# First channel product of six chunks by Strassen's algorithm, and reciprocals through rings, in an attention and mixer kernel

## The chip, the core and the metric

The kernel runs on one core of one Trainium2 chip. Its engines work side by side, each on its own list of instructions in order: PE (TensorE) multiplies matrices into the banks of PSUM, DVE (VectorE), ACT (ScalarE) and POOL (GpSimd) work on tiles, and SP issues transfers, as ACT and POOL do too. The time is device microseconds (us) of one execution; the number compared is the median of several.

## The reference

Eight batches of 576 positions by 8 heads of 64 go through an attention whose kernel is a random feature map, and then through a mixer over tokens and over channels.

```python
def phi(x):
    h = np.einsum('bhsd,md->bhsm', x, omega) - np.sum(x * x, axis=-1, keepdims=True) / 2.0
    return np.exp(h - np.max(h, axis=-1, keepdims=True)) / np.sqrt(m)
kv  = np.einsum('bhsm,bhsd->bhmd', phi(k_s), v)
z   = np.sum(phi(k_s), axis=2)
x   = einsum(phi(q_s), kv) / (einsum(phi(q_s), z) + 1e-06)      # attention, 8 x 576 x 512

u   = x + (np.maximum(xT @ w_tok1, 0.0) @ w_tok2)T              # tokens: 576 -> 256 -> 576
out = u + np.maximum(u @ w_ch1, 0.0) @ w_ch2                    # channels: 512 -> 1536 -> 512
```

## The kernel before

**Tiling.** Of a batch's 576 positions 512 are its main part; the 64 that are left of each of the eight batches make up a ninth chunk of 512, the tail. The channel part runs over nine chunks c: the batches 0 to 7 and the tail (c = B). Everything on PE is fp16 and is summed in fp32 in eight banks of 128 x 512.

**Order.** No scheduler decides at run time. The code adds jobs (an engine, a function, the jobs it waits for, the ring places it takes and gives back) to a `Planner`, and `ORDER`, a list of job numbers written out in the file, says in which order they are issued. `SLOT` gives the ring place (a bank, a buffer) for each job that takes one, `MOVED` the jobs that run on another engine than the usual one, and negative numbers in `ORDER` are matmuls on zeros at the start. So each engine's list, and what a ring place waits for, is fixed.

**Stages of a batch.** `load_transposed` casts q and k on POOL's queue into scratch memory and brings them back transposed on SP's queue into a place of the rings qT and kT (three each). `attention` projects k and q on PE (L656, L668), takes the exponential on ACT (L514), the maximum over features and its reciprocal on DVE (L680, L682), multiplies v by it on POOL (L295, `vs`), and forms the product of k's features and v (L701 to L710) and from it, for each head, numerator and denominator (L734, L736). One job (`num_out`) then takes the reciprocal of the denominator and scales the head into x (L743, L744); for two heads of batch 0 the scaling is on ACT instead (L756). `token_mix` makes two products with a relu between them (L777, L790) and adds x (L793); u is transposed by a transfer on SP's queue into uT (`ut_dma`, L798). The tail's rows are added for pairs of batches in `token_tail` (L850) and transposed into uTt.

**Channel part.** `channel_mix` makes the first product directly: for each of 12 blocks of 128 of the 1536 channels, 4 matmuls of 512 columns into one bank (L966), and a relu of that bank to fp16 (L290 on ACT, L292 on DVE). The second product is direct for batch 0 (L1000). For the other chunks `channel_out_fast` makes it by Strassen's algorithm in Winograd's form: four sums of quarters of the relu's output on DVE (L295, tiles S and r), four differences of quarters of the weights made once (T1 to T4), seven products of 24 matmuls of 256 columns (L916), and adds that read the banks into the output tile (L905), which a store then sends out (L945, L952).

Helpers that the profile names by their own lines: `copy` (L286), `relu_to` (L290, L292), `tt` (L295).

Of the kernel before, what the change touches and what calls it, by code (L numbers as in the profile page):

```python
# [9 lines left out]
FP32 = mybir.dt.float32  # L10
# [158 lines left out]
def kernel(  # L169
# [12 lines left out]
    nc = tc.nc  # L182
# [888 lines left out]
```

## Time and profile before

| | |
|---|---|
| Time, median of 3 | 276.59 us (276.38, 276.59, 277.32) |
| Span of the profiled execution, first to last instruction | 275.9 us |
| Instructions | 6228 |
| First product of the tail and most batches (L966), one matmul as the profile models its end | 379 ns |
| Bytes moved by transfers | 39.66 MB |

Only the span of the profiled execution is known, not its time as it is measured from outside; the difference to the median is 0.7 us. The profile gives the busy time of each engine, the same in stretches of time, groups of equal instructions (a line of the kernel, an engine, tiles without their numbers, shapes, a count, busy time and mean duration of one, and the idle time before them with what ended it), and the chain that ended last: from the last instruction back, at each step, to what released it. Matmuls are pipelined, so the duration of one is longer than the distance from one to the next.

### The profile page before, as it was taken

Reading aid. Unit: us, or ns where it says so; the run is one execution under the profiler, and the core shown is the slowest. Engines: PE = TensorE matmul, PEld = TensorE weight load, DVE = VectorE, ACT = ScalarE, POOL = GpSimd, SP = SyncE. Lnnn points to the kernel's source line nnn. Section 1 sums busy time; section 2 is a strip of 40 time slices with the busy share of each in tenths; the row PEclk is TensorE's granted clock in tenths of the full one; section 3 lists DMA queues with packets and bytes.
Section 4 is the critical chain, followed back from the end, with each engine's and each line's share of the span. In section 5 each row is a group of like instructions: output and inputs, shape, how many; then the busy total and the mean of one; then the engine's idle time right before and its main releaser. Section 6 shows DMA issues by size and latency. Waiting matters only on the chain.

```text
span 275.9 us, 6228 instructions
## 1 busy us (share of the span) xinstructions
PE 266.6 (97%) x2503; PEld 165.5 (60%) x2503; DVE 222.9 (81%) x462; ACT 138.1 (50%) x289; POOL 91.2 (33%) x115
## 2 busy tenths in 40 slices
PE   8789999999999999999999999999999999999993
PEld 3367455444567655755676656755676477446782
DVE  3897889876998799987999899978985992675992
ACT  3999941188685338734756456636654500040200
POOL 8994492063703490075019510600043000000001
PEclk9999999999999999999999999999999999999998
DMA  7999999999998999979989994840252304021125
GB/s 195 192 209 212 190 212 177 202 193 146 203 191 133 229 176 186 151 148 171 198 184 183 232 125 123 191 90 2 97 79 77 96 0 95 2 99 53 78 83 146
DMA packets 81292, 39.66 MB, mean 144 GB/s; under 512 B 63984, under 2 KB 77040, under 8 KB 81072
## 3 DMA queue, kind: packets, MB, share of 16 engines
q0 software_dynamic: 31744, 17.74, 44.2%
q1 hardware_dynamic: 47072, 15.50, 28.7%
q10 hardware_dynamic: 2448, 6.03, 5.6%
q8 instruction: 19, 0.31, 0.5%
q14 instruction: 9, 0.07, 0.1%
HBM read 35.95 MB, written 16.52 MB: 190 GB/s over the span
## 4 chain that ended last, share of the span: by engine, by line
PE 89%; DMA 6%; POOL 3%; DVE 0%; issue 0%; POOLq 0%
PE bank L966 33%; PE bank L916 25%; PE bank L777 5%; PE bank L790 5%; DMA w1m<-in_moe_w_tok_dram 4%; PE bank L1000 4%; PE bank L734 3%; PE bank L656 3%; PE bank L668 2%; PE bank L701 2%; DMA uT<-u 2%; POOL r L319 1%; PE bank L844 1%; PE bank L816 1%; PE bank L828 1%; PE bank L736 1%
## 5 line engine op out<-in xcount | busy, mean ns | idle before, releaser
L966 PE MATMUL bank<-uT,wc 128*128 128x512 f16 x376 | 90.4, 379 | 0.3 <-DMA uT<-u 0.3
L290 ACT ACTIVATE r<-bank 128x512 f16<-128x512 f32 (+1 forms) x84 | 46.9, 597 | 77.1 <-PE bank L966 62.0
L295 POOL TENSOR_TENSOR vs<-v,vs 128x512 f16<-128x512 f16 x31 | 33.2, 1074 | 91.2 <-DVE vs L682 60.5
L966 PEld LDWEIGHTS <-wc 128*128 128x128 f16 x424 | 38.3, 98 | 37.9 <-issue 1.1
L916 PEld LDWEIGHTS <-r 128*128 128x128 f16 x384 | 36.9, 98 | 8.1 <-issue 1.2
L514 ACT ACTIVATE kp<-bank 128x512 f16<-128x512 f32 x64 | 35.6, 622 | 10.4 <-PE bank L656 10.4
L514 ACT ACTIVATE qp<-bank 128x512 f16<-128x512 f32 x64 | 36.3, 616 | 8.9 <-PE bank L668 6.0
L680 DVE TENSOR_REDUCE km<-kp 128x8 f16<-128x1024 f16 x32 | 38.6, 1206 | 2.5 <-ACT kp L514 2.4
L292 DVE TENSOR_SCALAR r<-bank 128x512 f16<-128x512 f32 (+1 forms) x42 | 27.7, 672 | 12.0 <-PE bank L966 11.2
L744 DVE TENSOR_TENSOR x<-bank,rc 128x320 f16<-128x320 f32 x62 | 30.5, 492 | 2.1
L916 PEld LDWEIGHTS <-S 128*128 128x128 f16 x288 | 27.9, 98 | 5.4 <-issue 0.3
L905 DVE TENSOR_TENSOR o<-u,bank 128x512 f32<-128x512 f16 x28 | 19.0, 679 | 6.9 <-PE bank L916 6.8
L916 PE MATMUL bank<-T,r 128*128 128x256 f16 x192 | 23.8, 273 | 0.0
L916 PE MATMUL bank<-T,S 128*128 128x256 f16 x192 | 23.6, 273 | 0.0
L916 PE MATMUL bank<-wc,r 128*128 128x256 f16 x192 | 23.6, 273 | 0.0
L945 POOL DMA_DIRECT2D out_dram<-o x2 | 1.3, 648 | 60.9 <-issue 60.9
L793 DVE TENSOR_TENSOR u<-x,bank 128x512 f16<-128x512 f16 x28 | 17.8, 681 | 1.1 <-PE bank L790 1.0
L905 DVE TENSOR_TENSOR o<-o,bank 128x512 f32<-128x512 f32 (+1 forms) x27 | 16.6, 618 | 2.2 <-PE bank L916 1.6
L734 PEld LDWEIGHTS <-qp 128*128 128x128 f16 x256 | 13.8, 98 | 7.0 <-DVE kvsb L286 0.2
L734 PE MATMUL bank<-kvsb,qp 128*128 128x65 f16 x256 | 15.6, 193 | 0.0
L743 DVE RECIPROCAL rc<-bank 128x5 f32<-128x5 f32 x62 | 11.5, 186 | 4.1 <-PE bank L736 2.7
L701 PEld LDWEIGHTS <-kp 128*128 128x128 f16 x256 | 11.5, 98 | 5.1
(120 smaller groups left out, 376.3 us busy)
## 6 DMA issues: line engine op xcount, KB each, us to landing
out_dram<-o ACTq DMA_DIRECT2D x9, 512.0 KB, 2.6
q<-in_q_dram POOLq DMA_DIRECT2D x6, 576.0 KB, 7.2
wc<-in_moe_w_ch_dram POOLq DMA_DIRECT2D x4, 768.0 KB, 10.6
k<-in_k_dram POOLq DMA_DIRECT2D x6, 512.0 KB, 6.9
v<-in_v_dram POOLq DMA_DIRECT2D x6, 512.0 KB, 8.9
out_dram<-o SPq DMA_DIRECT2D x5, 512.0 KB, 3.9
r<-in_q_dram POOLq DMA_DIRECT2D x4, 288.0 KB, 7.3
v<-in_v_dram POOLq DMA_DIRECT2D x4, 256.0 KB, 8.7
```

Source lines behind the costliest of these rows:

```text
L290: nc.scalar.activation(out=out, in_=in_, func=AF.Relu)
L292: nc.vector.tensor_relu(out=out, in_=in_)
L295: (nc.gpsimd if eng == "POOL" else nc.vector).tensor_tensor(**kw)
L514: nc.scalar.activation(out=out, in_=in_, func=AF.Exp, bias=0.0, scale=1.0)
L680: nc.vector.reduce_max(out=mx, in_=kpv, axis=AX.X)
L701: nc.tensor.matmul(ps[:, i, :], kpv[:, 2 * i + j // 2, j % 2, :], vs[:, i * NJ + j, 0 : D + 1], start=(i == 0 and j == 0), stop=False, ski ...
L734: nc.tensor.matmul(ps[:, k, j * 65 : (j + 1) * 65], st, s[:, i, 0 : D + 1], start=True, stop=True)
L744: nc.vector.tensor_tensor(out=t_x[place("x", b)][:, :, (2 * hp + hs[0]) * D : (2 * hp + hs[0] + n) * D].rearrange("p j (i d) -> p i j d", ...
L793: nc.vector.tensor_tensor(out=t_u[place("u", b)][:, j, :], in0=t_x[place("x", b)][:, j, :], in1=bank(n), op=ALU.add)
L905: nc.vector.tensor_tensor(out=o, in0=a, in1=ps, op=ALU.add)
L916: nc.tensor.matmul(ps[:, j * DH : (j + 1) * DH], a[:, cb, j * P : (j + 1) * P], w[:, cb, :], start=(bank_of(b, j0) not in held and j == j0 ...
L966: nc.tensor.matmul(ps, wc1[:, db, cb * P : (cb + 1) * P], moving(db), start=(db == 0), stop=(db == ND - 1))
```

## The change

**First product.** From batch 3 on (`FAST_IN = 3`), and for the tail, the first channel product is made by Strassen's algorithm too. The two operands are split in quarters: channels in halves of 768, the 512 inputs in halves of 256 (k), the 512 positions in halves of 256 (j). `weight_sums` makes four sums of quarters of wc1 once, before batch 3's channel part; six of their eight halves lie in one place of the qT ring and one of the kT ring, which they hold to the end, two in a new tile. For each chunk four differences of quarters of uT are made into another place of uT's ring. For each of three groups of two blocks, seven products of four matmuls of 256 columns go into three banks X, Y and Z. A product that others go on adding to is first kept: ACT copies the bank in fp32 to a free buffer (r3, qp or kp), and DVE joins the kept sum with another bank (L1101 of the changed kernel). The relu of three quarters is then made in place in SBUF, that of the fourth from the bank.

```diff
+    FAST_IN = 3
...
+    def weight_sums(key):
+        def quad(i, k, a):
+            return wc1[:, 2 * k + a, i * (DC // 2) : (i + 1) * (DC // 2)]
+        steps = (((1, 0), (1, 1), ALU.add), (0, (0, 0), ALU.subtract), ((0, 0), (1, 0), ALU.subtract), ((0, 1), 1, ALU.subtract))
+        for a in range(2):
+            done = []
+            for i, (x, y, op) in enumerate(steps):
+                e_sum = engine("DVE")
...
+    def channel_in_fast(c, key, jt):
...
+        steps = ((lambda: block(0, 1), lambda: block(0, 0)), (lambda: block(1, 1), lambda: sums()[:, 0]), (lambda: block(1, 1), lambda: block(0, 1)),
+                 (lambda: block(1, 0), lambda: sums()[:, 1]))
...
+        ops = {
+            "P1": ("X", weights(0, 0), lambda: block(0, 0), []),
+            "P2": ("Y", weights(0, 1), lambda: block(1, 0), []),
+            "P5": ("Z", sum_weights(0), lambda: sums()[:, 0], [j_sums[0][0], j_sums[1][0], j_s[0]]),
+            "P6": ("X", sum_weights(1), lambda: sums()[:, 1], [j_sums[0][1], j_sums[1][1], j_s[1]]),
+            "P7": ("X", sum_weights(2), lambda: sums()[:, 2], [j_sums[0][2], j_sums[1][2], j_s[2]]),
+            "P4": ("X", weights(1, 1), lambda: sums()[:, 3], [j_s[3]]),
+            "P3": ("Z", sum_weights(3), lambda: block(1, 1), [j_sums[0][3], j_sums[1][3]]),
+        }
...
+                    for n in range(2):
+                        for a in range(2):
+                            nc.tensor.matmul(ps[:, n, :], w(a)[:, (2 * m + n) * P : (2 * m + n + 1) * P], x_[:, a],
+                                             start=(what in ("P1", "P2", "P5") and n == 0 and a == 0), stop=False, skip_group_check=True)
...
+            p1 = product("P1", [])
+            p2 = product("P2", [])
+            p5 = product("P5", [])
+            k1 = keep("P1", "X", p1)
+            c11 = join("P1", "Y", 0, 0, [k1, p2], True)
+            p6 = product("P6", [k1])
+            k2 = keep("U2", "X", p6)
+            p7 = product("P7", [k2])
+            k3 = keep("U3", "X", p7)
+            c22 = join("U3", "Z", 1, 1, [k3, p5, c11], False)
+            p3 = product("P3", [c22])
+            c12 = join("U2", "Z", 0, 1, [k2, p3], True)
+            p4 = product("P4", [k3])
...
     def channel_mix(c, key, jt):
         def moving(db):
             return (t_uT[place("uT", c)] if c < B else uTt)[:, :, db, :]
+        if c >= FAST_IN:
+            channel_out_fast(c, key, channel_in_fast(c, key, jt))
+            return
```

**Reciprocals.** What was one job is split: the maximum and its reciprocal, the reciprocal of the denominator and the scaling are jobs of their own, and their small results take places of rings (km 4, rc 8, kmt 2) instead of two fixed ones that alternate. The scaling can run on ACT for any head.

```diff
-    t_km = ring(2, [P, 8], FP16, "km")
-    t_kmt = ring(2, [P, 4], FP16, "kmt")
+    t_sum = sb([P, 2, DC // 2], FP16, "sum")
+    t_km = ring(COUNT["km"], [P, 8], FP16, "km")
+    t_kmt = ring(COUNT["kmt"], [P, 2, 4], FP16, "kmt")
-    t_rct = ring(2, [P, 4], FP16, "rct")
-    t_rc = ring(4, [P, 2, NJ + 1], FP32, "rc")
+    t_rc = ring(COUNT["rc"], [P, NJ + 1], FP32, "rc")
...
+                def rec(hp=hp, i=hs[0], where=where):
+                    nc.vector.reciprocal(out=t_rc[place("rc", (b, hp, i))], in_=where()[:, 0, 0 : 5 * 65].rearrange("p (j d) -> p j d", d=65)[:, :, D])
+                j_r = add("DVE", 0.1, kno, rec, deps=[j_n], take=[("rc", (b, hp, hs[0]))])
+                e_num = engine("DVE")
...
+                    if e_num == "ACT":
                         for j in range(NJ + 1):
+                            nc.scalar.activation(out=to[:, j], in_=ps[:, j], func=AF.Copy, scale=rc[:, j : j + 1])
+                    else:
+                        nc.vector.tensor_tensor(out=to, in0=ps, in1=rc.unsqueeze(2).broadcast_to((P, NJ + 1, D)), op=ALU.mult)
```

**Places and order.** The r1 ring has two places, not three. The tail's output is formed in places of the x ring instead of the output ring. Two more options (`SPLIT`, `HALVES`) are in the code and are empty. `ORDER`, `SLOT` and `MOVED` are new throughout; with them some sums of the second product, most sums of u and five weight sums run on POOL, eleven more heads are scaled on ACT, and the transposes of batches 5 to 7 stand at other places of SP's list.

```diff
-             "kvsb": 3, "ktt": 2, "x": 3, "r1": 3, "u": 3, "uT": 3, "r3": 2, "S": 1, "o": 2, "bank": 8}
+             "kvsb": 3, "ktt": 2, "x": 3, "r1": 2, "u": 3, "uT": 3, "r3": 2, "S": 1, "o": 2, "km": 4, "rc": 8, "kmt": 2, "bank": 8}
...
+        def o_tag(i):
+            return ("x", ("o", i)) if tail else ("o", (c, i))
```

More of the change, by code (lines that the diff above doesn't have):

```diff
@@ L104 @@
+    1318: "POOL", 1319: "POOL", 1320: "POOL", 1334: "DVE", 1351: "ACT", 1352: "ACT", 1391: "ACT", 1392: "ACT",
+    1397: "POOL", 1398: "POOL", 1430: "DVE", 1431: "ACT", 1447: "ACT",
 }
@@ L598, in kt_max @@
                 )
-            j_ktm = add("DVE", 1.2, kkt + 0.01, kt_max, deps=[*j_kte, j_msk], take=[("vbd", b)] if dma_in else [])
+            j_ktm = add("DVE", 0.15, kkt + 0.01, kt_mask, deps=[j_ktm, j_msk], take=take_vbd, give=[("kmt", b)])
             def vbd():
@@ L762, in attention @@
+                last_x.append(add(e_num, 0.45, kno, scale, deps=[j_r], take=[("x", b)], give=[at, ("rc", (b, hp, hs[0]))]))
         return last_x
@@ L865, in channel_out_fast @@
             part = slice(g * NH // 2, (g + 1) * NH // 2)
-            need = [jr[cb + NH * e] for cb in range(part.start, part.stop) for e in range(2)]
+            need = [x for cb in range(part.start, part.stop) for e in range(2) for x in jr[cb + NH * e]]
             steps = (
@@ L897, in bank_of, with o_of, go @@
             return (b, c, j0) if tail else (b, c)
+        def o_tag(i):
+            return ("x", ("o", i)) if tail else ("o", (c, i))
+        def o_of(i):
+            if tail:
+                return t_x[place(*o_tag(i))].rearrange("p j d -> p (j d)")[:, 0 : 4 * DM].bitcast(FP32).rearrange("p (j d) -> p j d", j=2)
+            return t_o[place(*o_tag(i))]
         def read(k, b, i, e, base, deps, free, j0=0, j1=2):
-            def go(c=c):
-                o = t_o[place("o", (c, i))][:, j0:j1, DH * e : DH * e + DH]
+            e_read = engine("DVE")
+            def go(c=c, e_read=e_read):
+                o = o_of(i)[:, j0:j1, DH * e : DH * e + DH]
                 ps = bank(bank_of(b, j0)).rearrange("p (j d) -> p j d", j=2)[:, j0:j1]
+                if e_read == "ACT":
+                    nc.scalar.copy(out=o, in_=ps)
+                    return
                 u = t_u[place("u", c)] if c < B else t_ut
@@ L944, in store @@
                         to = out[4 * i : 4 * i + 4, SM:S, cols].rearrange("(j h) t d -> h t j d", h=2)[h]
-                        (nc.scalar if eng == "ACT" else nc.sync if eng == "SP" else nc.gpsimd).dma_start(out=to[:, js], in_=t_o[place("o", (c, i))][half[h], js, cols])
-                    dma(eng, key + 0.9, 0.3, store, deps=[outs[need, j] for j in range(*js)], give=[("o", (c, i))],
+                        (nc.scalar if eng == "ACT" else nc.sync if eng == "SP" else nc.gpsimd).dma_start(out=to[:, js], in_=o_of(i)[half[h], js, cols])
+                    dma(eng, key + 0.9, 0.3, store, deps=[outs[need, j] for j in range(*js)], give=[o_tag(i)],
                         cost=0.412 if js[1] - js[0] == 1 else 0.414)
@@ L951, in store @@
             def store(i=i, eng=eng):
-                (nc.scalar if eng == "ACT" else nc.sync).dma_start(out=out[c, 0:SM, :].rearrange("(p j) d -> p j d", j=NJ)[:, 2 * i : 2 * i + 2, :], in_=t_o[place("o", (c, i))])
-            dma(eng, key + 0.9 + 0.1 * i, 1.3, store, deps=[outs[x, 0] for x in need], give=[("o", (c, i))], cost=0.4)
+                (nc.scalar if eng == "ACT" else nc.sync).dma_start(out=out[c, 0:SM, :].rearrange("(p j) d -> p j d", j=NJ)[:, 2 * i : 2 * i + 2, :], in_=o_of(i))
@@ new lines, in channel_out_fast, with sum_of, go @@
+            dma(eng, key + 0.9 + 0.1 * i, 1.3, store, deps=[outs[x, 0] for x in need], give=[o_tag(i)], cost=0.4)
+    j_sums = []
+    def sum_of(i, k):
+        n = 2 * i + k
+        if n < 6:
+            tag = "qT" if n < 3 else "kT"
+            return (t_qT if n < 3 else t_kT)[place(tag, "sums")][:, n % 3 * (DC // 2) : n % 3 * (DC // 2) + DC // 2]
+        return t_sum[:, n - 6]
+    def weight_sums(key):
[3 more added lines that the diff above has]
+        for a in range(2):
+            done = []
+            for i, (x, y, op) in enumerate(steps):
+                e_sum = engine("DVE")
+                def go(i=i, a=a, x=x, y=y, op=op, e_sum=e_sum):
+                    x, y = [sum_of(z, a) if isinstance(z, int) else quad(*z, a) for z in (x, y)]
+                    tt(e_sum, out=sum_of(i, a), in0=x, in1=y, op=op)
+                need = [done[z] for z in (x, y) if isinstance(z, int)]
+                n = 2 * i + a
+                done.append(add(e_sum, 0.46, key, go, deps=[*need, *j_wc1], take=[("qT" if n < 3 else "kT", "sums")] if n < 6 else []))
+            j_sums.append(done)
@@ L984, in relu @@
                 relu_to(e_relu, t_r3[place("r3", c)][:, cb, :], bank(n))
[L985 removed]
+            jr[cb] = [add(e_relu, 0.5, key + 0.5 * pos / NCB, relu, deps=[j1], take=[("r3", c)], give=[("bank", n)])]
         if fast:
```

201 lines of the change are left out of this document (144 added, 57 removed), and 132 rows, old and new, of the table ORDER.

## The prediction

> **What bounds the kernel now.** I read the page's head first, then the stretches of time, then the chain that ended last, and only then the groups.
>
> ```profile
> span 275.9 us, 6228 instructions
> ...
> PE 266.6 (97%) x2503; PEld 165.5 (60%) x2503; DVE 222.9 (81%) x462; ACT 138.1 (50%) x289; POOL 91.2 (33%) x115
> ...
> PEclk9999999999999999999999999999999999999998
> ...
> PE 89%; DMA 6%; POOL 3%; DVE 0%; issue 0%; POOLq 0%
> ```
>
> The page's head shows one engine at 97% and a chain that runs 89% over it. Whether those 97% are real work is told by the stretches (columns: PE, PEld, DVE, ACT, POOL busy us, granted clock, DMA share, GB/s).
>
> ```profile
> 0.00:10.00 10.00, 7.51 (x82) 4.08 (x82) 4.82 (x18) 5.27 (x10) 8.55 (x19) 1.00 0.91 189
> 10.00:20.00 10.00, 8.39 (x150) 4.75 (x151) 9.12 (x20) 9.67 (x28) 9.50 (x12) 1.00 1.20 207
> 20.00:30.00 10.00, 9.54 (x162) 7.06 (x155) 7.70 (x18) 9.34 (x23) 4.00 (x6) 1.00 1.22 205
> 30.00:50.00 20.00, 20.00 (x167) 10.28 (x165) 18.25 (x37) 9.61 (x21) 11.73 (x13) 1.00 1.28 192
> 50.00:70.00 20.00, 20.00 (x174) 9.93 (x172) 14.37 (x26) 13.41 (x28) 7.06 (x9) 1.00 1.09 178
> ...
> 130.00:150.00 20.00, 20.00 (x206) 13.97 (x205) 18.86 (x38) 12.13 (x26) 5.82 (x7) 1.00 1.05 186
> ...
> 270.00:276.00 6.00, 1.44 (x14) 1.05 (x11) 1.27 (x3) 0.00 (x0) 1.15 (x2) 0.82 0.51 135
> ```
>
> From 30 us on PE has no idle time until 271.4, at full granted clock; what it lacks is lost in the first 30 us and in the last 4.5, where only stores are left. A busy PE need not be an efficient one, so I took two long unbroken pieces of the chain of waits (start, us, what):
>
> ```profile
> 234.09 13.81 PE bank L966 x64
> ...
> 260.94 10.51 PE bank L916 x96
> ```
>
> 64 matmuls of 512 columns in 13.81 us are 0.2158 us each; 96 of 256 columns in 10.51 are 0.1095. Half the columns take half the time although each has its own weight load, so a matmul costs its columns and nothing else, and time can only be saved by fewer columns on PE.
>
> **The change on PE.** The direct first product (L966) is 48 matmuls of 512 columns a chunk: 48 x 0.2158 = 10.36 us. By Strassen a chunk takes 3 groups x 7 products x 4 matmuls = 84 of 256 columns: 84 x 0.1095 = 9.20. That is 1.16 us less, and for six chunks (batches 3 to 7 and the tail) 7.0 us less. PE gets nothing else new. Bounds: the moving operand is now strided over two blocks, but L966's was strided too, so I keep the row's price; if each of the 504 cost 5 ns more, 2.5 us would go.
>
> **The other engines.** The rows that price what is added and removed:
>
> ```profile
> L290 ACT ACTIVATE r<-bank 128x512 f16<-128x512 f32 x82 | 46.1, 602 | 76.6 <-PE bank L966 62.0 <-PE bank L777 8.9 <-DVE o L905 5.4
> ...
> L295 POOL TENSOR_TENSOR vs<-v,vs 128x512 f16<-128x512 f16 x31 | 33.2, 1074 | 91.2 <-DVE vs L682 60.5 <-PE bank L668 22.3 <-PE bank L966 4.5
> ...
> L744 DVE TENSOR_TENSOR x<-bank,rc 128x320 f16<-128x320 f32 x62 | 30.5, 492 | 2.1
> ...
> L292 DVE TENSOR_SCALAR r<-bank 128x512 f16<-128x512 f32 x40 | 26.9, 684 | 11.7 <-PE bank L966 11.2
> ...
> L905 DVE TENSOR_TENSOR o<-o,bank 128x512 f32<-128x512 f32 x21 | 14.1, 674 | 1.6 <-PE bank L916 1.1 <-issue 0.2
> ...
> L295 DVE TENSOR_TENSOR S<-r,S 128x768 f16<-128x768 f16 x16 | 8.5, 553 | 0.2
> ...
> L286 DVE CAST kvsb<-bank 128x130 f16<-128x130 f32 x12 | 3.4, 287 | 5.1 <-PE bank L708 5.1
> ...
> L756 ACT ACTIVATE x<-bank,rc 128x64 f16<-128x64 f32 x10 | 2.3, 340 | 0.0
> ...
> L295 POOL TENSOR_TENSOR T<-vt,T 128x1024 f16<-128x1024 f16 x1 | 1.9, 1941 | 0.0
> ...
> L286 ACT COPY o<-bank 128x512 f32<-128x512 f32 x2 | 1.3, 638 | 4.8 <-PE bank L1000 4.8
> ...
> L290 ACT ACTIVATE r<-bank 128x256 f16<-128x256 f32 x2 | 0.8, 384 | 0.4 <-PE bank L817 0.4
> ...
> L545 DVE COPY ktt<-kT 128x256 f16<-128x256 f16 x1 | 0.2, 227 | 0.0
> ```
>
> Counts come from the two instruction lists.
>
> DVE gains 54 joins of a kept product with a bank, priced as L905's add: 54 x 0.674 = 36.4; 3 relus from a bank at 0.684, 2.1; 3 weight sums at 0.553, 1.7; 6 sums of u of 512 elements, between the copy's 0.227 and 0.553, taken as 0.42 = 2.5; 10 relus in place of 512 elements and 8 of 1024, never seen: below by 0.227 each, above by 0.684 per 512 (17.8 in all); nearest are the fp16 rows, so 0.30 and 0.45 = 6.6. It loses 24 relus (16.4), 17 sums for the second product, given to POOL (9.4), 11 scalings of heads, given to ACT (5.4), and 2 casts (0.6). Net 49.3 - 31.8 = +17.5, so 240.4.
>
> ACT gains 54 keeps x 0.638 = 34.5; 15 relus at 0.602 = 9.0; 55 scalings (11 heads of 5) x 0.340 = 18.7; 8 relus in place at 0.602 and 10 of twice that size at 1.04 (0.602 plus twice the 0.218 between 256 and 512) = 15.2; 2 casts, taken at 0.287; it loses 48 relus, 28.9. Net +49, so 187.
>
> POOL gains 18 sums of u at 1.074 and 22 of 768 elements, between 1.074 and 1.941, taken half-way at 1.5: 19.3 + 33 = 52, so 143.5.
>
> Against a span near 269 these are 89, 70 and 53%. No engine overtakes PE, but DVE has much less air. How much less is a question of how the count of durations relates to time on a full engine (timeline of DVE and ACT: start, us, what):
>
> ```profile
> 106.99 0.56 DVE L295 TENSOR_TENSOR S<-r,S 128x768 f16<-128x768 f16 x1
> 107.47 0.55 DVE L295 TENSOR_TENSOR S<-S,r 128x768 f16<-128x768 f16 x1
> ...
> 108.53 0.68 DVE L793 TENSOR_TENSOR u<-x,bank 128x512 f16<-128x512 f16 x1
> 109.13 0.55 DVE L295 TENSOR_TENSOR S<-r,S 128x768 f16<-128x768 f16 x1
> ```
>
> ```profile
> 202.38 0.59 ACT L514 ACTIVATE kp<-bank 128x512 f16<-128x512 f32 x1
> 202.85 0.60 ACT L514 ACTIVATE qp<-bank 128x512 f16<-128x512 f32 x1
> ```
>
> Back to back, DVE starts the next instruction 0.08 us before the last one is through (0.48 after a 0.56, 0.60 after a 0.68), ACT 0.12 before. So durations overstate the load: the 480 or so DVE instructions need about 38 us less than their sum.
>
> **Waits that the change adds.** Four products of a group share bank X (P1, P6, P7, P4) and two bank Z: before the next one adds to a bank, ACT must have kept, or DVE joined, the last sum. In PE's new order I added up the matmuls that stand between each product and the next on its bank: at the least 0.87 us of other PE work, four places under 1.1, half of them over 2.8. A keep takes 0.638. So nearly all handoffs are covered; if the cover were gone each would cost about 0.64, and behind a waiting product stands everything in PE's queue. I count 0.3 for the thin ones.
>
> The transposes by DMA have less lead. Priced by the trace's landing times (queue, count, median us from issue to landing):
>
> ```profile
> uT<-u SPq DMA_TRANSPOSE x7, 5.4
> kT<-k SPq DMA_TRANSPOSE x6, 5.6
> qT<-q SPq DMA_TRANSPOSE x6, 6.1
> ```
>
> Six of the eight weight sums now hold one of three places of qT and of kT from before batch 5's load on, so batches 5 to 7 load later. PE work between issue and first use, counted the same way, is 5.5 us for batch 7's qT against 6.1 to land: 0.6 late. For u it was 6.0 to 8.0 and becomes 5.0 to 5.7 from batch 4 on, against 5.4: I take 0.4 in all, 0 to 2 as bounds. The first sums of u come behind that, but P1 and P2 need none.
>
> At the end, from the last transpose of u to the last matmul, PE has 43.9 us (43.3 before), DVE 79 instructions of 44.4 us (55 of 31.7 before). Less 79 x 0.08 it is 38.1, 87% of PE's. Before, DVE there waited for PE; now the last relus, sums and reads come in a close chain, with only batch 7's last 12 matmuls (1.3 us) as cover between the tail chunk's two products. I take 0.7, with 0 and 3 as bounds.
>
> **Edits at nothing.** The reciprocals and scalings are split into jobs of their own and go through rings of 4 and 8 places: the same 64 and 32 instructions, on an engine that is not on the path. The tail's output now lies in x's places: same adds, same stores. The first 70 us of PE, SP and POOL are the same but for bank numbers and a few swaps, so the head keeps its 4.6 us of idle time. r1 has two places in the room of three; in the new order each pair's tail product, which frees them, still stands ahead of the next token product, so nothing waits. What hides the split is the air of DVE above; without it the instructions would still be the same ones, and only their order on a full DVE would count (the first rival).
>
> **The sum.** 275.9 - 7.0 + 0.3 + 0.6 + 0.4 + 0.7 = 270.9 of span. The median shown is 276.59, 0.7 over this execution's span, and I keep that difference: **271.6 us**.
>
> **A rule that speaks against it.** POOL's sums and DVE's run side by side now (timelines of DVE and of POOL):
>
> ```profile
> 14.52 1.02 DVE L295 TENSOR_TENSOR vs<-v,vs 128x512 f16<-128x512 f16 x1
> ```
>
> ```profile
> 13.39 1.05 POOL L295 TENSOR_TENSOR vs<-v,vs 128x512 f16<-128x512 f16 x1 [0.47 <-DVE vs L682]
> ...
> 14.96 1.50 POOL L295 TENSOR_TENSOR vs<-v,vs 128x512 f16<-128x512 f16 x1
> ```
>
> The one POOL multiply that ran into a DVE one with both inputs in SBUF took 1.50 instead of 1.05. The Trainium skill, "GPSIMD Engine Reference", section "Key points", says that POOL shares its SBUF interfaces with VectorE and is held up by DVE instructions with two SBUF inputs; the trace agrees, 0.45 us for 0.58 of overlap. In the sum: 77 adds on POOL, 0.45 each at worst, are 35 us on an engine with 125 to spare; it moves no term, only the lateness of sums, which is the third rival.
>
> **Rivals.**
> - **DVE becomes the bound.** Busy DVE time is 54.3 up to 70 us and 168.6 after; with 17.5 more it is 186.1 for the 199 us left, 93.5%. The densest row above, 130 to 150, reached 94.3%. If dependences hold it to 92%, the rest takes 202.3: 70 + 202.3 + 0.7 = 273.0; at 90%, 206.8: 277.5. Against it: the 0.08 of overlap.
> - **No net gain by late sums and transposes.** Every transpose at its slowest landing, and POOL sums at 1.94 with 0.45 of contention in chains of four: 4 us more on the path, 275.6.
> - **Slower: the handoffs are exposed.** 18 groups with 3 keeps on bank X, if ACT, now with 54 keeps and 55 scalings in one queue, reaches them late. At 0.64 each with half of the 54 exposed: 17.3, so 276.6 - 7.0 + 17.3 = 286.9; a third, 281.1. It decides from 7.0 / 54 = 0.13 us a handoff. For it: no such chain is in the trace; against it, the counted cover.
>
> **How the numbers follow.** The forecast (269.2 to 273) has 0.60, the DVE bound 0.18, late sums 0.08, exposed handoffs 0.14. The low end is the pure sum, 269.6, with a little less head; the high end, 276.5, takes in most of the second and third case and leaves the slower one out. A change of 0.3% (0.8 us) is about what can be told from none. Faster by more: 0.60, 0.12 of the second and 0.05 of the third, 0.77; the same 0.06; slower 0.17.
>
> **What would show it.** Right: PE's busy time near 259 to 260 and still full from 30 us to 266; the new first product at 0.11 us a matmul in the chain; DVE near 240, ACT near 187; no wait of PE on ACT or DVE above 1 us in total for the new line. Wrong: PE idle in the stretches after 90 us, with PE waiting for a keep, a join or a transpose; joins longer than 0.68; DVE busy 20 of 20 in several stretches.

## The result and the profile after

| | before | after |
|---|---|---|
| Time, median of 4 executions on one chip | 276.54 us (276.38 to 277.32) | 286.04 us (285.30 to 286.62) |
| Span of the profiled execution | 275.9 us | 284.1 us |

The ratio is 1.0314, with a 95% interval of 1.0287 to 1.0342: slower by 9.5 us, where 5 us less were forecast. Below, "faster" and "slower" go by such ratios against the kernel before, measured on the same chip in the same session; in some experiments single executions were disturbed and longer by several us, which the ratios leave out, but the profiles of e1, e6, e9, e13 and e16 are of such executions. In the experiments the kernel's line numbers differ by up to eight.

From the page of the changed kernel, its head, the granted clock and the engines of the chain that ended last:

```profile
span 284.1 us, 6855 instructions
...
PE 265.0 (93%) x2719; PEld 188.3 (66%) x2719; DVE 237.5 (84%) x492; ACT 175.3 (62%) x385; POOL 146.7 (52%) x155
...
PEclk9899999999999999999998999999999999999998
...
PE 72%; DMA 13%; DVE 7%; ACT 3%; POOL 2%; issue 2%; DVEq 0%; POOLq 0%
```

The sums of DVE and POOL came out near the forecast (240.4 and 143.5), ACT's 12 us under it (187), but the chain is no longer PE's alone: DMA rose from 6% to 13%, and DVE, 0% before, has 7%. Where PE is not full is told by the stretches of time (PE, PEld, DVE, ACT, POOL busy us, granted clock, DMA share, GB/s):

```profile
90.00:110.00 20.00, 18.84 (x183) 10.53 (x182) 17.70 (x36) 14.62 (x39) 17.85 (x18) 1.00 0.85 155
110.00:130.00 20.00, 16.89 (x196) 13.42 (x196) 19.20 (x36) 10.73 (x26) 16.08 (x15) 1.00 0.89 153
130.00:150.00 20.00, 17.37 (x168) 12.38 (x166) 17.48 (x36) 13.72 (x30) 8.68 (x9) 0.96 1.17 178
150.00:170.00 20.00, 20.00 (x236) 16.74 (x235) 16.62 (x39) 14.46 (x36) 12.52 (x14) 0.95 0.84 153
170.00:190.00 20.00, 17.92 (x186) 12.91 (x185) 16.81 (x33) 14.63 (x33) 12.30 (x12) 1.00 0.93 125
...
250.00:270.00 20.00, 20.00 (x186) 17.92 (x184) 20.00 (x41) 9.85 (x16) 0.00 (x0) 1.00 0.14 59
```

After the first 30 us PE is idle only between 90 and 230, in a few places. The end, where DVE is busy 20 of 20, is full on PE too: the tail, feared in the forecast, is not where the time went. What ended PE's waits there (engine and line, what it waited for, us in all, times, longest):

```profile
PE bank L575 <- DMA kT<-k: 2.6, 1, 2.6
PE bank L1077 <- ACT x L788: 2.5, 1, 2.5
PE bank L965 <- DVE u L823: 1.6, 1, 1.6
PE bank L739 <- POOL vs L319: 1.6, 1, 1.6
PE bank L1077 <- DMA uT<-u: 1.5, 2, 1.0
PE bank L695 <- DMA qT<-q: 0.2, 1, 0.2
```

For the kernel before the same question, from 90 to 230 us, has an empty answer. (A little earlier, at 89 us, PE waits there for a transpose of u, for 0.3 us; the forecast's "no idle time" from 30 us on passes over it.) Six rows, 10.0 us, seven waits: no keep (L310) and no join (L1101) is among them. Two kinds are: behind DVE (4.1 us; the scaling on ACT at 125 us stood behind a DVE reciprocal) and behind transfers (5.9 us; POOL's multiply `vs` at 179 us stood behind the cast of v).

**The waits behind DVE.** The timelines of DVE and POOL around the two places (start, us, engine, line):

```profile
103.97 1.26 POOL L375 DMA_DIRECT2D vt<-in_v_dram  x2
104.29 0.55 DVE L319 TENSOR_TENSOR kT<-wc 128x768 f16<-128x768 f16 x1
104.76 3.10 DVE L319 TENSOR_TENSOR S<-r 128x768 f16<-128x768 f16 x1
105.19 0.57 POOL L388 DMA_DIRECT2D k<-in_k_dram  x1
105.75 1.68 POOL L319 TENSOR_TENSOR r<-r 128x768 f16<-128x768 f16 x1
107.78 1.21 DVE L716 TENSOR_REDUCE km<-kp 128x8 f16<-128x1024 f16 x1
...
119.69 0.42 DVE L319 TENSOR_TENSOR uT<-uT 128x512 f16<-128x512 f16 x1
120.15 0.65 POOL L375 DMA_DIRECT2D vt<-in_v_dram  x1
120.23 3.63 DVE L319 TENSOR_TENSOR uT<-uT 128x512 f16<-128x512 f16 x1
120.82 1.17 POOL L319 TENSOR_TENSOR uT<-uT,uT 128x512 f16<-128x512 f16 x1
121.93 1.64 POOL L319 TENSOR_TENSOR sum<-wc,qT 128x768 f16<-128x768 f16 x1
```

A DVE sum that takes 0.55 lasts 3.10, one that takes 0.42 lasts 3.63, and both end 0.3 to 0.4 us after a POOL sum does. DVE's queue, with the adds of u and the reciprocals in it, is 2.55 and 3.21 us late, and PE's two waits follow.

**The half clock.** After the longest wait (kT, PE goes on at 147.99) two equal rows of PE's timeline, 12 matmuls of 256 columns each, and one of the new first product:

```profile
148.44 2.74 PE L965 MATMUL bank<-wc,r 128*128 128x256 f16 x12
...
153.86 1.48 PE L965 MATMUL bank<-T,S 128*128 128x256 f16 x12
...
183.06 1.92 PE L1077 MATMUL bank<-uT,wc 128*128 128x256 f16 x16 [0.52 <-DMA uT<-u]
```

From 148.5 to 151.9 us the granted clock is half (the 0.96 and 0.95 of the stretches), and matmuls take twice the time: 3.4 us at half are 1.7 us more, which no wait shows. The head of the changed kernel has such a stretch too, from 11.9 to 15.3 us (same columns as the stretches above):

```profile
10.00:20.00 10.00, 8.81 (x109) 3.95 (x106) 7.84 (x16) 8.90 (x23) 8.43 (x10) 0.83 1.20 204
```

The kernel before has 1.00 there. Batch 1's transpose of u goes out at 55.5 us, against 54.9 in the kernel before and 54.1 in the version without casts further down (e10), whose clock is full there. Of the traces of the other versions three have half clock in the head (e11, e15 and e18); whether the change brings it is not shown.

### The profile page after: what moved, and what is told of

It is laid out like the page before. It is cut to its first block, busy times and chain, and to the rows that moved or that the text cites. A ratio compares the mean times of both kernels' runs of the same rounds, so it can differ in the third digit from the quotient of the medians.

```text
span 284.1 us, 6855 instructions
## 1 busy us (share of the span) xinstructions
PE 265.0 (93%) x2719; PEld 188.3 (66%) x2719; DVE 237.5 (84%) x492; ACT 175.3 (62%) x385; POOL 146.7 (52%) x155
## 4 chain that ended last, share of the span: by engine, by line
PE 72%; DMA 13%; DVE 7%; ACT 3%; POOL 2%; issue 2%; DVEq 0%; POOLq 0%
PE bank L965 20%; PE bank L1077 18%; PE bank L1148 10%; DMA uT<-u 5%; PE bank L1182 4%; DMA kT<-k 4%; PE bank L807 3%; PE bank L772 2%; DMA qT<-q 2%; PE bank L820 2%; DMA r<-in_q_dram 2%; PE bank L739 2%; PE bank L683 2%; PE bank L695 2%; DVE km L716 2%
## 5 line engine op out<-in xcount | busy, mean ns | idle before, releaser
L314 ACT ACTIVATE r<-bank 128x512 f16<-128x512 f32 (+1 forms) x51 | 29.6, 600 | 17.4 <-PE bank L807 7.7
L1148 PE MATMUL bank<-uT,wc 128*128 128x512 f16 x136 | 32.9, 379 | 0.0
L1077 PE MATMUL bank<-uT,wc 128*128 128x256 f16 x192 | 25.8, 273 | 4.1 <-ACT x L788 2.5
L790 DVE TENSOR_TENSOR x<-bank,rc 128x320 f16<-128x320 f32 x51 | 24.5, 484 | 1.0
L1077 PEld LDWEIGHTS <-wc 128*128 128x128 f16 x216 | 20.3, 98 | 7.4 <-DMA uT<-u 1.8
L945 DVE TENSOR_TENSOR o<-o,bank 128x512 f32<-128x512 f32 x21 | 14.1, 673 | 7.5 <-PE bank L965 7.2
L319 POOL TENSOR_TENSOR vbd<-vt,vbd 128x512 f16<-128x512 f16 x6 | 6.3, 1058 | 27.0 <-DVE vbd L620 14.5
L1148 PEld LDWEIGHTS <-wc 128*128 128x128 f16 x136 | 12.0, 97 | 12.2 <-issue 1.1
L1077 PE MATMUL bank<-uT,kT 128*128 128x256 f16 x108 | 18.9, 272 | 0.0
L1077 PE MATMUL bank<-uT,qT 128*128 128x256 f16 x108 | 18.5, 273 | 0.0
L310 ACT COPY r<-bank 128x512 f32<-128x512 f32 x18 | 10.3, 596 | 13.1 <-PE bank L1077 12.7
```

The lines of the kernel that those rows point to most:

```text
L310: (nc.scalar.copy if eng == "ACT" else nc.vector.tensor_copy)(out=out, in_=in_)
L314: nc.scalar.activation(out=out, in_=in_, func=AF.Relu)
L319: (nc.gpsimd if eng == "POOL" else nc.vector).tensor_tensor(**kw)
L790: nc.vector.tensor_tensor(out=to, in0=ps, in1=rc.unsqueeze(2).broadcast_to((P, NJ + 1, D)), op=ALU.mult)
L945: nc.vector.tensor_tensor(out=o, in0=a, in1=ps, op=ALU.add)
L1077: nc.tensor.matmul(ps[:, n, :], w(a)[:, (2 * m + n) * P : (2 * m + n + 1) * P], x_[:, a], start=(what in ("P1", "P2", "P5") and n == 0 and ...
```

## The experiments

Theory A: POOL and DVE shut each other out. Theory B: DVE is the bound. Theory C: keeps come late. Theory D: transfers land late.

**Three sums back on DVE.** Jobs 476, 604 and 610 are the three POOL sums of the timeline above.

```diff
 MOVED = {
...
-    476: "POOL",
-    604: "POOL",
-    610: "POOL",
```

> Of the changed kernel only three sums go from POOL back to DVE: one of batch 2's second product (r<-r, which began at 105.75 us) and the two that began at 120.82 and 121.93 us (uT<-uT,uT and sum<-wc,qT). They are the POOL sums that run straight behind DMA issues while a DVE sum lasts 3.10 and 3.63 us instead of 0.55 and 0.42. Theory A (POOL and DVE shut each other out while both read two SBUF inputs, and these two collisions cause PE's stalls of 1.74 us at 110.4 and 2.70 at 125.2): both stalls go, about 4.4 us back, 286.0 -> 281.6. Theory B (DVE is the bound): DVE gets 0.55 + 0.42 + 0.55 = 1.5 us more, so no gain, 286 to 287.5. Theory C (exposed keeps and ACT late): nothing of the keeps is touched, 286.0.

Measured: 1.0135 (1.0061 to 1.0209), executions from 279.5 to 286.5 us: 1.8% under the changed kernel's ratio, 5.0 us, by the two intervals give or take about 2. No DVE sum is held any more, and the waits behind u and x are gone. The profiled execution has a wait of 3.6 us for batch 3's kT at 82 us, with half clock after it, that the changed kernel's profile lacks. From 90 to 230 us PE's waits are:

```profile
PE bank L1078 <- DMA uT<-u: 3.6, 4, 1.8
PE bank L740 <- POOL vs L320: 2.8, 1, 2.8
PE bank L576 <- DMA kT<-k: 1.2, 1, 1.2
PE bank L696 <- DMA qT<-q: 0.2, 1, 0.2
```

Only transfers are left (`vs` waits for v's cast). Theory A accounts for these 5.0 us of the loss; B is refuted as it was put, since a fuller DVE was faster.

**All sums back on DVE.** All 40 entries for POOL go out of `MOVED`.

> All 40 sums that the changed kernel has on POOL go back to DVE at their places in the order. POOL then has only its multiplies for v (about 38 of them). DVE gets 22 x 0.55 + 18 x 0.42 = 19.7 us more, busy about 254 of 284. Theory A (collisions): collisions with sums can't happen any more, 4.4 us back at least, less what the fuller DVE costs: 279 to 283. Theory B (DVE is the bound): its busy time was 84% in the changed kernel; with 19.7 more it sets the pace, slower than 286.0 by up to 10: 289 to 296. Theory C: 286 or a little more.

Measured: 1.0394 (1.0348 to 1.0441), 287.9 us. The page's head:

```profile
PE 266.0 (93%) x2719; PEld 187.9 (66%) x2719; DVE 248.6 (87%) x532; ACT 175.6 (61%) x385; POOL 91.9 (32%) x115
```

No sum is held for long, yet PE waits 3 us for DVE in short waits (adds of o, u, uT, S) beside 7 for transfers. So the sums on POOL are not the mistake by themselves: with all of them on DVE it is late often and by little, and with them on POOL it is late twice, but then by 3 us.

**The heads back on DVE.** Eleven entries for ACT (567, 581, 584, 716 and so on, the scalings of batches 3 to 7) go out of `MOVED`.

> Of the changed kernel only the eleven heads' scalings that ACT took over (five instructions of 0.34 each) go back to DVE, one of 0.49 each: ACT loses 18.7 us, DVE gets 5.4. Theory C (ACT has too much and keeps come late): 3 us or more back, 280 to 283. Theory B (DVE is the bound): 5 us slower, 291. Theory A: within 1 us of 286.0, or the stall of 2.70 us at 125.2, where PE waits for scalings that ACT makes behind a delayed DVE, changes by less than 1.

Measured: 1.0355 (1.0317 to 1.0392), 287.1 us. Both held sums are there (2.80 and 3.62 us), and PE waits 3.4 us after the second. ACT with 11 us less to do gains nothing: theory C falls.

**The exclusion by itself.** A kernel of its own: stretches of DVE and POOL work with a barrier between them.

```python
    p_sum(6)          # POOL: pc = pa + pb, 768 columns
    d_sum(20)         # DVE: dc = da + db, 768 columns
    barrier()
    p_dma(4)          # POOL: cast transfers
    d_sum(12)
    barrier()
    for _ in range(3):
        p_dma(2)
        p_sum(1)
    d_sum(24)
    ...
```

> A kernel of its own, which writes zeros as its output: stretches of 768-column fp16 sums on DVE (two SBUF inputs, alone 0.55 us) beside, in turn, nothing, POOL sums of the same size (alone 1.64), POOL's cast transfers, and POOL's transfers followed by one sum; then, beside POOL sums, DVE adds with one input in PSUM, DVE maxima over 1024 elements and DVE copies. Theory A (exclusion: whoever has begun keeps the other out for the whole instruction): beside POOL sums a DVE sum lasts 0.55, or 0.55 and most of a POOL sum, 2.2, and nothing between dominates; the 20 DVE sums beside 6 POOL sums need about 20 x 0.55 + 6 x 1.6 = 20 us rather than 10; a DVE sum begun while POOL issues its last transfer ahead of a sum lasts over 2; beside transfers alone DVE's sums stay at 0.55. A rival for the mechanism (sharing at a lower rate): DVE sums of 0.7 to 1.2 throughout and POOL sums of 2 to 2.5, no long single ones. The maxima aren't held under either.

Groups of equal instructions, by stretch (count, busy us, mean ns): DVE sums alone; six beside six POOL sums, and these; beside POOL's transfers; adds with one input in PSUM, maxima, and copies beside POOL sums; copies alone.

```profile
L65 DVE TENSOR_TENSOR dc<-da,db 128x768 f16<-128x768 f16 x10 | 5.6, 558 | 0.3
...
L65 DVE TENSOR_TENSOR dc<-da,db 128x768 f16<-128x768 f16 x6 | 11.4, 1894 | 0.2
...
L69 POOL TENSOR_TENSOR pc<-pa,pb 128x768 f16<-128x768 f16 x6 | 10.8, 1794 | 0.5
...
L65 DVE TENSOR_TENSOR dc<-da,db 128x768 f16<-128x768 f16 x11 | 6.1, 558 | 0.3
...
L99 DVE TENSOR_TENSOR u<-x,bank 128x512 f16<-128x512 f16 x14 | 9.6, 687 | 0.5
...
L103 DVE TENSOR_REDUCE km<-kp 128x8 f16<-128x1024 f16 x8 | 9.8, 1219 | 0.2
...
L107 DVE COPY dc<-da 128x768 f16<-128x768 f16 x6 | 10.2, 1698 | 0.2
...
L107 DVE COPY dc<-da 128x768 f16<-128x768 f16 x17 | 6.1, 360 | 0.6
```

A DVE sum of 0.56 lasts 1.89 beside POOL sums, the two in turn; PSUM adds, maxima and POOL's transfers cost nothing. It is exclusion, not sharing. This is what the Trainium skill states in "SBUF — State Buffer", section "Who interferes with whom": whoever comes first has the shared pair for the whole instruction, and DVE instructions with two SBUF inputs contend with POOL's reads. The trace agrees. And where a sum follows POOL's transfers (timeline):

```profile
56.71 2.58 DVE L65 TENSOR_TENSOR dc<-da,db 128x768 f16<-128x768 f16 x1
56.71 0.49 POOL L76 DMA_DIRECT2D s<-in_k_dram  x1
57.22 1.64 POOL L69 TENSOR_TENSOR pc<-pa,pb 128x768 f16<-128x768 f16 x1
```

DVE is held from 56.71, half a us before the recorded start of the POOL sum, and for 2.02 us in all: the pattern of 104.76 and 120.23.

**Batch 6's k earlier.** Fragments of `ORDER`, here and below:

```diff
-    ..., 619, 620, 1041, 766, ... 661, 665, 1040, 873, ... 881, 780, 1043, 903, ...
+    ..., 768, 633, 1041, 1040, 610, ... 869, 871, 1043, 498, ...
```

> Of the changed kernel only the order of three transfers is changed: batch 6's casts of k stand ahead of the POOL sums that began at 120.8 us (they were issued at 131.8), and its transpose (issued at 137.7, landed 10.2 later, PE waited 2.80 us for it at 148.0) stands on SP's list ahead of batch 2's two stores (132.95). Theory D (late transfers are a second, independent cause): the stall at 148.0 goes, 2.8 us back, 283.2; if POOL's sums are then later and something else lands late, 284 to 286. Theories A, B and C by themselves: 286.0, since the lost time is then caught up elsewhere.

Measured: 1.035 (1.0313 to 1.0387), 287.6 us. The wait for kT is gone; instead PE waits 1.6 us for qT and 6.1 for uT, with 6.8 us at half clock behind the longest. One DVE sum is still held (3.40 us), and PE waits 3.4 us in all for DVE's u and o. The gain was eaten in the next transposes.

**Batch 6's v earlier**, with the three sums on DVE:

```diff
-    ..., 815, 894, 1046, 802, ...
+    ..., 909, 812, 1046, 1222, ...
```

> As the run with three sums back on DVE, and the one cast transfer of batch 6's v (issued at 169.4 us in the changed kernel, behind a wait of POOL, and after batch 7's v) stands ahead of batch 7's, some 8 us earlier. PE waited 1.7 us at 179.2 in the changed kernel and 2.98 at 180.2 in the run with three sums back, for POOL's multiply behind that transfer. Theory D (late transfers are the second cause): that wait goes, 1.7 to 3 us less than the run with three sums back (which gave 279.5 to 283.3): about 279. Theory A alone: no change against it.

Measured: 1.0211 (1.0153 to 1.0269), 282.3 to 288.3 us. The wait for v went; but POOL, whose `vbd` now stood behind two loads of v, made the sums S late by 3.9 us, and uT of batch 5 came 3.3 late.

**All casts of batches 5 to 7 earlier**, with three sums and with all 40 on DVE (jobs 862, 868, 1039 to 1041, 1046, 1215 to 1217 moved ahead of POOL's sums, 1043 ahead of the stores):

> As the run with three sums back on DVE, and all casts of k, q and v of batches 5 to 7 that need no place wait for nothing: they stand some 5 to 35 us earlier on POOL's list, ahead of its sums, and batch 6's transpose of k ahead of batch 2's stores. Theory D (late transfers): PE's waits for kT at 147, uT at 155, v at 180 and qT at 200 go, in all 5 to 6 us: 275 to 277. If instead the transfers only crowd each other (transfers' engines full), the waits move to other transposes and the time stays at 280 to 284.

> All 40 POOL sums on DVE, as before (287.9), with the same earlier casts. Theory D: 4 to 6 us less than 287.9, 282 to 284. Theory B (with the sums DVE is the bound): no change, 287 to 288.

Measured: 1.0420 (1.0363 to 1.0477) and 1.0445 (1.0405 to 1.0485). The first is clearly slower than without the move (1.0135); the second (1.0394 without) lies within overlapping intervals, but gains nothing. In the first a small DVE multiply (0.19 us) that began while POOL issued a cast was held for 3.69, over two POOL sums, and PE waited 2.9 us for the add of u behind it and 5.8 for uT. Theory D, in the form that an earlier place is enough, fell here twice.

**The casts left out.** If the transfers' load makes the transposes late, they must come in time without it:

```diff
             def cast(w=w):
+                if b >= 5:
+                    return
...
-                nc.sync.dma_start_transpose(out=t.unsqueeze(1), in_=scratch[w, b])
+                nc.sync.dma_start_transpose(out=t.unsqueeze(1), in_=scratch[w, min(b, 4)])
```

With three sums on DVE, with the sums as in the changed kernel, and in the kernel before:

> As the run with three sums back on DVE, with the casts of q and k of batches 5, 6 and 7 left out (their transposes read batch 4's copy): 3.4 MB less for the transfers, the same work on PE, ACT and DVE. Theory A with D (collisions and late transfers together make the loss): PE's waits for kT, qT and uT fall to near those of the kernel before (0.5 us in all), 272 to 275. If PE still waits 5 us or more for uT or for other engines, the transfers' load is not the second cause: 278 to 282.

> The changed kernel with its POOL sums where they are, and with the same casts of batches 5 to 7 left out. Without them POOL comes to its sums earlier and by another way, so collisions may fall elsewhere. Theory A: if DVE sums of over 2 us are in the trace, each costs PE 1.7 to 2.7 us, 276 to 280; if none is, the time is that of the run without casts with three sums back, 272 to 275. Theory D alone: 272 to 276, whatever the DVE sums last.

> The kernel before, with the same casts of q and k of batches 5, 6 and 7 left out (their transposes read batch 4's copy). PE has no idle time there from 30 to 271 us, so if the load of the transfers costs something in the changed kernel alone (theory D), this changes nothing: within 1 us of the kernel before, 0.997 to 1.001. If the casts' load slows any kernel, it is faster by some 4 to 6 us, as the changed one is without them.

Measured: 0.9887 (0.9866 to 0.9908), 274.3 us; 0.9974 (0.9946 to 1.0001), 276.4 us; 1.0024 (1.0006 to 1.0042), 277.7 us. The kernel before gains nothing, the changed one with three sums back 2.5% (6.9 us), and the changed one as it is 3.4% (9.4 us). In the first, the whole list of PE's waits between 90 and 230 us is

```profile
PE bank L1084 <- DMA uT<-u: 1.9, 2, 1.0
```

and there is no half clock from 5 us to the end. The second differs from it by 0.87%, 2.4 us; in its trace two DVE sums are held, by 1.50 and 0.97 us. So the price of each cause depends on the order: with the three sums put back first they are worth 5.0 us and the casts then 6.9; with the casts left out first these are worth 9.4 and the sums then 2.4.

Leaving casts out takes more away than load. SP's queue, which issues the transposes, held those of k of batches 5 and 6 in the changed kernel for 6.6 and 1.6 us, until k's cast had landed, and POOL issues fewer transfers. These runs don't part such effects from the load. A transpose of u waits for no cast; two of them, of batches 4 and 5, took 4.7 and 4.8 us to landing in the kernel before, 8.4 and 7.5 in the changed one, and 4.7 and 6.1 without casts and with three sums back. Transposes of u between 100 and 200 us, count and median us to landing, of the kernel before, the changed one, the one with three sums back, and that without casts:

```profile
uT<-u SPq DMA_TRANSPOSE x4, 5.1
```
```profile
uT<-u SPq DMA_TRANSPOSE x3, 7.5
```
```profile
uT<-u SPq DMA_TRANSPOSE x3, 8.7
```
```profile
uT<-u SPq DMA_TRANSPOSE x4, 5.7
```

The transposes of k and q show no such rise: in the same order of kernels their medians are 5.8, 5.1, 6.5 and 6.6 for k, and 5.9, 6.6, 7.3 and 5.7 for q.

**The loads in another order**, with all the work done and three sums on DVE: batch 6's transfers put right (e9), in order of use (e13), batch 7's spread (e14), and that with batch 6's k (e15). The first fragment is e9's, the second e14's.

```diff
-    ..., 664, 672, 1039, 920, ... 909, 812, 1222, 888, ... 889, 1051, 1044, 945, ... 815, 894, 1046, 802, ...
+    ..., 936, 1045, 1044, 1046, 805, ... 785, 935, 1039, 1217, ... 947, 1216, 1222, 1059, ...
```

```diff
-    ..., 820, 928, 1215, 798, ... 816, 947, 1216, 1059, ... 962, 1079, 1219, 1118, ...
+    ..., 935, 1217, 1216, 821, ... 909, 812, 1046, 888, ... 1091, 1042, 1219, 951, ... 1116, 1215, 1222, 1221, 1056, ...
```

> As the run with three sums back on DVE (279.5 to 283.3, 1.3% over the kernel before), and five transfers at other places of POOL's list: batch 6's v and the last part of its v tails ahead of batch 7's v (in the runs so far POOL's vbd of batch 6 stood 4 to 10 us for that tail, behind batch 7's v), batch 6's q behind uT's landing instead of beside it, and the second part of batch 6's k one sum earlier. Theory D (the second cause is transfers that POOL's list issues late or beside a transpose): PE's waits for kT at 147 (1.3), uT at 155 (1.9) and v at 180 (3.0) go: 6 us less, 274 to 277. If they move: 279 to 283.

> As the run with three sums back on DVE, with the transfers on POOL's list put in the order of their use: batch 6's last v tail and q ahead of the sum that waits for uT, batch 6's v at the place of batch 7's, batch 7's v behind all loads of batch 6, the second part of batch 6's k one sum earlier. Theory D, if it is the order of the loads that makes them late: PE's waits for v at 180 (3.0 us) and for uT at 155 (1.9) go, 275 to 278. If it is their amount (the transfers' engines are nearly full until 170 us, and whatever is put first delays another), other waits of the same size take their place: 279 to 284.

> As the run with three sums back on DVE, with batch 7's loads taken out of the crowd around u's transpose at 175 us: its k is cast with the first part at 155 and transposed ahead of that transpose, its q and v are cast only after 178; batch 6's v takes the place of batch 7's. If lateness can be mended by spreading the loads: the waits for v at 180 (3.0 us) and uT at 184 (0.6) go, 277 to 279; if the loads only crowd another transpose: 280 to 284.

> The same, and batch 6's k: its second part one sum earlier and its transpose ahead of batch 2's two stores. If lateness can be mended by spreading: the waits for kT at 147 (1.3) and uT at 155 (1.9) shrink too, 275 to 277, which would beat both kernels; if it is the amount of the transfers up to 170 us: 279 to 284.

Measured: 1.0251 (1.0200 to 1.0302); the second scattered from 280 to 305 us and has no ratio; 1.0317 (1.0249 to 1.0385); 1.0371 (1.0348 to 1.0394). The wait for v at 180 us went in all four (0.4 us of it is left in e9), that for uT at 155 in e9 and e13, that for kT in e15. Others came or grew: e9 waited 8.8 us for qT behind the moved cast (the transpose landed 16.5 us after its issue) and 1.2 for kT, e13 3.1 for qT and 4.5 for uT, e14 5.2 and e15 7.2 for uT.

**u's transpose in two halves** (e16), with batch 7's loads spread (e17), and these loads two POOL operations later (e18):

```diff
-            nc.sync.dma_start_transpose(
-                out=t_uT[place("uT", b)].rearrange("p j a c -> p (j a) c"),
-                in_=t_u[place("u", b)].rearrange("p j d -> p (j d)"),
-            )
+            for i in range(2):
+                nc.sync.dma_start_transpose(
+                    out=t_uT[place("uT", b)][:, 2 * i : 2 * i + 2].rearrange("p j a c -> p (j a) c"),
+                    in_=t_u[place("u", b)][:, 2 * i : 2 * i + 2].rearrange("p j d -> p (j d)"),
+                )
```

> As the run with three sums back on DVE, with u's transpose of batches 1 to 7 sent as two transfers of half the positions each, one behind the other on SP's list; the first two products of a group need only the first half. In the run with three sums back PE waited 3.6 us for uT in all between 90 and 230 us. If the transposes' length is what makes uT late: the first half lands some 2 us earlier, the wait falls to 1.5 or less, 2 us less time. If the crowd of transfers is: the first half lands as late as the whole did, no gain, and 1 us more of issuing on SP ahead of the transposes of k and q.

> The same halves with batch 7's loads spread as before (283 to 287 without halves, PE's waits for uT there 5.2 us): if halves help, 3 us less, 280 to 283; if not, 283 to 287 again.

> As the run with halves and batch 7's loads spread (281.6), with batch 7's q, v and last v tail two of POOL's operations later: in that run POOL came to them at 170.0 us, while u's transpose of batch 6 (issued at 167.9) was on its way and landed 10 us later, and PE stood 3.07 us for the sum behind it, after which its clock was at half for 3.4 us. If the crowd at that place is the cause: both go, 3.1 + 1.7 = 4.8 us less, 276.8 to 278, level with the kernel before. If not, 281 to 283.

Measured: 1.0312 (1.0250 to 1.0375), 1.0153 (1.0133 to 1.0173) and 1.0163 (1.0131 to 1.0195). With halves PE's wait for uT falls to 0.5 us in e16, whose gain went to v, kT and qT (6.1, 3.2 and 2.6 us), and to none in e17, which at 281.6 us is level with e1 (1.0135), these two being the best of those that do all the work. PE's waits in e17 from 80 us on (the first row is the sum that needs the second half of batch 5's u):

```profile
PE bank L1079 <- DVE uT L320: 2.9, 1, 2.9
PE bank L576 <- DMA kT<-k: 1.6, 1, 1.6
PE bank L740 <- POOL vs L320: 1.3, 1, 1.3
PE bank L967 <- POOL S L320: 1.1, 1, 1.1
```

In e18 the first of these went as expected (the transpose that its expectation calls batch 6's is batch 5's), and in its profile a wait of 3.6 us for batch 3's kT at 83 us, with 3.4 us of half clock, stood in its place. No version that does all the work came below the kernel before.

## Why the prediction was wrong

**The change on PE: right.** The 16 matmuls of the row at 183.06, less the 0.27 us that one is recorded with, are (1.92 - 0.27) / 15 = 0.110 us apart (0.1095 forecast), and PE is full where nothing is late. Without collisions and casts (e10) the span is 271.7, 0.8 over the 270.9 of the sum. The sum has 2.0 us for waits, and the two waits for uT that are left take 1.9, so they don't explain the 0.8. One sign did not come: PE's busy time, forecast near 259 to 260, is 261.3 there and 265.0 in the changed kernel. Of the 261.3, 1.4 us more than in the kernel before fall in the first 30 us (26.8 against 25.4); the changed kernel has its half clock besides.

**The other engines: right but for ACT,** whose sum was forecast at 187 and came to 175.3. Joins, keeps and POOL's sums of the changed kernel (groups: count, busy us, mean ns, idle before):

```profile
L1101 DVE TENSOR_TENSOR r<-kp,bank 128x512 f16<-128x512 f32 x18 | 12.2, 676 | 0.1
...
L310 ACT COPY qp<-bank 128x512 f32<-128x512 f32 x18 | 10.6, 594 | 7.8 <-PE bank L1077 5.6 <-PE bank L772 1.6 <-DVE r L1101 0.7
...
L319 POOL TENSOR_TENSOR S<-r,S 128x768 f16<-128x768 f16 x6 | 9.9, 1642 | 0.0
```

against 674, 638 and 1500 forecast. The rival that DVE becomes the bound showed only in part, when all sums come back to it (3 us of PE's waits). Exposed handoffs, a rival with the right sign, showed in no list of waits of the changed kernel, and the counted cover was enough; that its 286.9 lies near the measured 286.0 is luck. The forecast's sign that the new line would wait for ACT or DVE no more than 1 us did not come: L1077 waited 2.5 us for ACT's scaling, which stood behind the held DVE.

**"A rule that speaks against it" failed.** The step took from the one overlap in the trace of before that POOL is the one delayed, by 0.45 us an add, and said it "moves no term". The row was read in one direction only: there DVE had begun first. In the changed kernel POOL had (in both places ahead of its recorded start, as the last section shows), and DVE, with PE behind it, lost 2.55 and 3.21 us. Putting three sums back was worth 5.0 us, where I had 0. I had also thought of POOL's sums as standing where `ORDER` has them; POOL runs ahead as soon as its waits allow, so which DVE instruction a sum meets isn't in the lists.

**"Waits that the change adds" failed for the transfers.** It priced every transpose by the landing times of before (5.4, 5.6, 6.1 us), and only those of u and batch 7's q: 0.4 and 0.6 us. In the loaded stretch they took longer (7.5 for u), kT of batch 6 and v of batch 6 were not in the sum at all, and waits for transfers came to 5.9 us. What a shorter PE does to every transfer's lead, and an added POOL sum to every cast behind it, was not asked. The rival "no net gain by late sums and transposes" had the mechanism, at 4 us and a chance of 0.08. With the casts left out of the kernel with three sums back 6.9 us came back. That this is the load is argued and not shown alone: it rests on the landing times of u and on the orders that moved the wait, and leaving casts out also frees the transposes of k from waiting for them.

**The half clock was in no term:** in the profiled execution 1.7 us from 148.5 us, and the stretch in the head, up to 1.4 us by batch 1's transpose of u (55.5 against e10's 54.1).

**The sum as it came out:** in ratios, from 0.982 (forecast) to 1.031 are 4.9%, 13.7 us: 5.0 for the collisions (give or take 2), 6.9 for the casts with the half clock behind their waits, and 1.8 left over. In the other order the two are 2.4 and 9.4, with about as much left over. Of the 1.8, 1.1 is the difference between time and span, which I took as 0.7 from two different executions; each execution measured since stands 1.7 to 2.0 over its own span.

Open: why batch 3's kT, whose order the change hardly touches, lands late in some executions of the later versions (e1, e16, e18) and in none shown of the kernel before; how much of the casts' 6.9 us is load and how much the waits of k's transposes for their casts; and why the changed kernel has half clock in its head.

## What to carry to other kernels

Before work goes to POOL, look at what DVE does at that time: an instruction with two inputs in SBUF (or an fp16 copy) on one is a lock for the other, and POOL's place in time is set by its waits, not by the order list. When the busy engine gets less work, go through every transfer that it waits for and price it by its slowest landing under load, not by its median. And price a wait of the matrix engine of about 3 us or more with the half clock that can follow it (1.7 us here for 3.4 at half).

## What was not expected of the hardware

The lock begins before the POOL sum's recorded start when POOL comes straight from issuing transfers: by 0.51 us in the kernel made for it, 0.99 at 104.76 and 0.59 at 120.23. There DVE, and the small multiply of e7, didn't get their turn between two POOL sums either, while with sums alone the two took turns. fp16 copies with a single SBUF input are held too (1.70 instead of 0.36 us).

Over the traces of all runs, from 30 us on, distances between two matmuls that were up to 2.75 us beyond the usual were never followed by half clock, those above 3.3 always, those between sometimes (2.79 was, 3.29 was not), for 3.4 us or twice that. The Trainium skill, "TensorE: Matmul & The Clock Gate", section "What's actually happening", has the clock set by a free-running window of about 3.4 us; the two durations agree with that, and so does it that the length of the wait alone doesn't decide.
